# K through a bf16 staging tile, and W2 loaded behind the transposes of chunk 1, in a two-layer attention and MLP kernel

## The chip, the cores and the metric

The kernel runs on one core of a Trainium2 chip. The metric is the device time of one execution in microseconds (us). Five engines work beside each other, each on its own queue in order: PE (TensorE, matmuls; its weight loads are shown apart as PEld), DVE (VectorE), ACT (ScalarE), POOL (GpSimd) and SP (SyncE, which here only issues DMAs). DVE and ACT read PSUM, where matmuls leave their results; POOL works on SBUF alone. A measurement of this kernel can tell about 0.3% from no change.

## The reference

Two blocks, A (attention in a sliding window) and B (an MLP), each on a layer norm of x and added to x, applied as A, B, A, B. x is 2048 rows by 512, in bf16. Cut to what matters:

```python
def _A_ref(x, wqkv, wo):           # H = 32 heads, Dh = 16, window W = 256
    q, k, v = split(x @ wqkv)      # (heads, 2048, 16) each
    scores = einsum("bhqd,bhkd->bhqk", q, k) * Dh ** -0.5
    mask = (i - j >= 0) & (i - j < W)
    p = softmax(where(mask, scores, -1e9))
    return einsum("bhqk,bhkd->bhqd", p, v) @ wo
def _B_ref(x, w1, w2):             # 512 -> 1792 -> 512
    return relu(x @ w1) @ w2
x = x + _A_ref(_layernorm(x), A_wqkv, A_wo)
x = x + _B_ref(_layernorm(x), B_w1, B_w2)
x = x + _A_ref(_layernorm(x), A_wqkv, A_wo)
x = x + _B_ref(_layernorm(x), B_w1, B_w2)
```

## The kernel before

**Chunks and steps.** The 2048 rows are four chunks of 512. With two layers that makes eight steps, k = 0 to 7; step k is chunk k % 4 of layer k // 4. In each step the rows are normed, transposed, multiplied into Q, K and V, attended to, multiplied by wo, added to x, normed again, transposed, and sent through w1, relu and w2.

**K and its spread.** K of a step is made transposed, as four tiles t of 128 channels (8 heads of 16) by 512 keys. A score matmul contracts 32 channels, that is two heads, and must keep their scores apart. So K is stored twice in the tile `KBD`: once with the odd heads' channels set to zero, once with the even ones'. `spread_k` (L324) does this with a per-partition factor `par` of 0 or 1: two instructions for a tile of 512 keys, that read the matmul's PSUM result in fp32 and write bf16 into slots of 64 keys. There are 20 slots, used in a ring; where a tile goes over the ring's end, each of the two instructions becomes two of 256 keys. In step 0 the rows come in two halves, and its K instructions cover 256 keys.

**V.** V is copied from PSUM into a bf16 staging tile `Vst` on DVE or ACT, and from there `spread_v` (L336) lays it out by parity into `V2f` on POOL or DVE. The staging tiles come from the pool `stg`, which has three buffers; the output rows `ob` of layer 1 use the same pool.

**Attention.** Scores of a group go to PSUM (`Sps`), ACT takes their exponential into `Pb`, masks are set to zero in `Pb` on POOL (`affine_select`, two instructions per block) or DVE (`min` with `tri`), and PE multiplies the result by V (`acc`). DVE divides (`chk`, `O`). The four DMA transposes `OT<-O` then bring O back to the layout for wo. The normed rows `xn` (three buffers, on DVE or POOL) are turned by DMA transposes, too: `xnT<-xn` for Q, K, V and `xn2T<-xn` for w1. In step 0, and in the last step behind O and its norm, PE does the transposes.

**Who orders the work.** Nothing is issued in the order of the source. Every piece of work is an `op` with a key (its urgency), the engines that may do it with a cost for each, and the ops it waits for. A small event loop in the kernel's Python (`choose`, `begin`, L718 to L757) gives each free engine the best op that it may start, and so writes the program: one fixed queue per engine, and the engine for each op. On the chip the queues then run in this order, and an engine that waits holds everything behind it. Where the loop sees PE idle it puts in a `warm` matmul with no use for its result. PE's results pass through four PSUM buffers (the pool `psum`); a buffer comes free when its last reader is done. K, Q and V of step k + 1 are due 16 score groups ahead of that step's first scores.

**Loads.** All loads are issued by SP at the start, in this order: x of chunk 0 in two parts, wqkv in three, x of chunks 1 to 3, wo, w1, w2. The two weights of the MLP, 1792 KB each, are both called `w` in the profile. Behind the loads stand SP's transposes, chunk 1's four `xnT<-xn` first. All of them use one DMA queue, spread over 16 DMA engines.

All instructions that the loop places are recorded by one helper and so carry its line, L106; they are told apart by their tiles.

Of the kernel before, what the change touches and what calls it, by code (L numbers as in the profile page):

```python
# [10 lines left out]
BF16 = mybir.dt.bfloat16  # L11
I32 = mybir.dt.int32
AX = mybir.AxisListType
ACT = mybir.ActivationFunctionType
ALU = mybir.AluOpType
P = 128
# [46 lines left out]
def kernel(  # L63
# [51 lines left out]
    pe, dve, act, pool, sp = (InOrder(x) for x in (nc.tensor, nc.vector, nc.scalar, nc.gpsimd, nc.sync))  # L115
# [23 lines left out]
    w1 = const.tile([P, KC, DFF], BF16, name="w1")  # L139
    sp.dma_start(w1[:], B_w1.rearrange("(kc p) n -> p kc n", p=P))  # L140
    w2 = const.tile([P, NF, D], BF16, name="w2")
    sp.dma_start(w2[:], B_w2.rearrange("(f p) n -> p f n", p=P))


    ident = const.tile([P, P], BF16, name="ident")
# [9 lines left out]
    par = const.tile([P, 2], FP32, name="par")  # L155
# [31 lines left out]
    SOON = {"qkv": 0, "v": 0, "h": 0, "mask": 0, "div": -1, "add": -1}  # L187
# [34 lines left out]
    def op(key, opts, deps=(), take=None, uses=(), keep=0):  # L222
        uses = list(uses) + ([take] if take is not None and take not in uses else [])
        return Op(key, opts, deps, take, uses, keep)
# [3 lines left out]
    stg = Pool("stg", 3, work)  # L228
    ots = Pool("OT", 3, work)

    def landed(t):
        o = Op(0, {}, [], None, [], 0)
        fixed.append((o, t))
        return o
# [2 lines left out]
    d_x = [landed(3.95), landed(4.5)]  # L237
    d_w = {1: landed(7.4), 0: landed(9.0), 2: landed(10.6)}
    d_xc = {c: landed(11.4 + 1.7 * c) for c in range(1, NCH)}
    d_wo, d_w1, d_w2 = landed(18.0), landed(24.0), landed(30.0)  # L240


    def copy(e, o, i, relu=False):
        if e == "ACT":
            act.activation(o, i, ACT.Relu if relu else ACT.Copy)
        elif e == "POOL":
            pool.tensor_copy(o, i)
        elif relu:
            dve.tensor_relu(o, i)
        else:  # L250
            dve.tensor_copy(o, i)
# [3 lines left out]
    def options(times, fn):  # L255
        return {e: (t, lambda e=e: fn(e)) for e, t in times.items()}
# [67 lines left out]
    def spread_k(e, layer, c, t, h0, h1, ps):  # L324
        s0 = slot(layer, 8 * c)
        for a, b in ([(h0, h1)] if s0 + h1 <= NSLOT or s0 + h0 >= NSLOT else [(h0, NSLOT - s0), (NSLOT - s0, h1)]):
            sa = (s0 + a) % NSLOT
            for p in range(2):
                o = KBD[:, t, sa:sa + b - a, p, :]
                i = ps[:, 64 * a:64 * b].rearrange("p (s k) -> p s k", k=64)  # L330
                if e == "ACT":
                    act.activation(o, i, ACT.Copy, scale=par[:, p:p + 1])
                else:
                    dve.tensor_scalar(out=o, in0=i, scalar1=par[:, p:p + 1], scalar2=None, op0=ALU.mult)

    def spread_v(e, layer, c, j, src):  # L336
        v4 = src.rearrange("p (a e d) -> p e a d", e=2, d=16)
# [124 lines left out]
    def plan_qkv(k):  # L462
        layer, c = divmod(k, NCH)
        xnTs[k] = xnT = [None]
        src = [x_raw(4 * c + j, 4 * c + j + 1)[:, 0, :] if layer == 0 else x_sb[:, 4 * c + j, :] for j in range(4)]
        lid = 2 * k
        st, dst = [], []
        calm = (-10, 1, 40, 60)[k] if k < 4 else 0
        for j in range(4):
            came = [d_x[j // 2] if c == 0 else d_xc[c]] if layer == 0 else [x_done[k - 4, j]]  # L470
            st.append(norm_stats(lid, j, src[j], came + applied.get(lid - 8, []), j - 1 if j % 2 else None, calm))
        pw = [norm_pow(lid, j, j + 2, [st[j], st[j + 1]], calm - 5) for j in (0, 2)]
        free = [] if k == 1 else qkv_mm.get(k - 1, []) + (qkv_mm[0] if k == 2 else [])

        class Late:
            def __getitem__(self, i):
                if xnT[0] is None:
                    xnT[0] = work.tile([P, KC, 512], BF16, name="xnT", tag="hT" if k == 1 else "xnT", bufs=1)
                return xnT[0]
        for j in range(4):  # L480
            dst.append(norm_apply(lid, j, src[j], [pw[j // 2]], k == 0, Late(), -5000, free))
        applied[lid] = list(dst)
        mine = qkv_mm[k] = []
        old = [scores[s] for n in units_of.get(k - 2, []) for s in range(first_slot[n], first_slot[n] + len(units[n].groups))]
        old_pv = [pvs[n, j] for n in units_of.get(k - 2, []) for j in range(units[n].nq // 2)]
        wait = 0 if k == 0 else 16
        for h in range(2) if k == 0 else (None,):
            cols = slice(0, 512) if h is None else slice(256 * h, 256 * h + 256)
            h0, h1 = (0, 8) if h is None else (4 * h, 4 * h + 4)
            us = 0.216 if h is None else 0.115  # L490
            need_x = dst if h is None else dst[2 * h:2 * h + 2]
            w = 512 if h is None else 256
            for t in range(4):
                at = first_slot[units_of[k][t + 4 * (h or 0)]] - wait
                idx = 4 * k + t

                def kmm(kc, ps, t=t, cols=cols):
                    mm(ps[:, cols], wqkv[:, kc, D + t * P:D + (t + 1) * P], xnT[0][:, kc, cols], kc == 0, kc == KC - 1)
                box, m = group(at, KC, us, kmm, need_x + [d_w[1]] + old[len(old) * t // 4:len(old) * (t + 1) // 4], lead=1000)
                times = {"DVE": 1.46, "ACT": 1.42} if h is None else {"DVE": 0.87, "ACT": 0.83}  # L500
                k_done[k, t, h or 0] = op(SOON["qkv"], options(times, lambda e, t=t, h0=h0, h1=h1, box=box:
                                                      spread_k(e, layer, c, t, h0, h1, box.ps)),
                                          [m, c_par], None, [box])

                def qmm(kc, ps, t=t, cols=cols):
                    mm(ps[:, cols], wqkv[:, kc, t * P:(t + 1) * P], xnT[0][:, kc, cols], kc == 0, kc == KC - 1)
                last_use = [scores[s] for n, u in enumerate(units) if 4 * u.k + u.t == idx - 7
                            for s in range(first_slot[n], first_slot[n] + len(u.groups))]
                box, m2 = group(at + 0.1, KC, us, qmm, need_x + [d_w[0]] + last_use, lead=1000)

                def qev(e, t=t, cols=cols, box=box, idx=idx):
                    q = first(Q, (k, t), lambda: work.tile([P, 512], BF16, name="Qt", tag=f"Q{idx % 7}", bufs=1))
                    copy(e, q[:, cols], box.ps[:, cols])
                q_done[k, t, h or 0] = op(SOON["qkv"], options(EVAC[w], qev), [m2], None, [box])
                mine += [m, m2]
        for j in range(4):
            at = first_slot[units_of[k][0]] + (1 + (8 if j > 1 else 0) if k == 0 else 1.6 * j - wait)

            def vmm(kc, ps, j=j):
                mm(ps[:], xnT[0][:, kc, j * P:(j + 1) * P], wqkv[:, kc, 2 * D:3 * D], kc == 0, kc == KC - 1)  # L520
            box, m = group(at + 0.2, KC, 0.216, vmm, ([dst[j]] if k == 0 else dst) + [d_w[2]] + old_pv, lead=1000)
            vs = Box(stg)

            def vev(e, box=box, vs=vs):
                vs.t = vs.tile([P, 512], BF16, "Vst")
                copy(e, vs.t[:], box.ps[:])
            ev = op(SOON["qkv"], options(EVAC[512], vev), [m], vs, [box, vs])
            v_done[k, j] = op(SOON["v"], options({"POOL": 1.72, "DVE": 1.42} if k else {"POOL": 1.72, "DVE": 1.42, "ACT": 1.48}, lambda e, j=j, vs=vs: spread_v(e, layer, c, j, vs.t[:])),
                              [ev] + c_v, None, [vs])
            mine.append(m)  # L530
# [142 lines left out]
    for k in range(NSTEP):  # L673
        plan_attention(k)
        if k == 0:
            plan_qkv(1)
        plan_rest(k)
        if 0 < k < NSTEP - 1:
            plan_qkv(k + 1)
# [32 lines left out]
        push(t, None, None)  # L712
    started, score_end, idle_since, log = set(), [0.0], [1.9], []
    score_next = [0]

    by_name = {"PE": pe, "ACT": act, "DVE": dve, "POOL": pool, "SP": sp}

    def choose(e, t):  # L718
        best = None
# [153 lines left out]
    with tc.If(flag > 0):  # L873
# [13 lines left out]
        for layer in range(2):  # L887
            for c in range(NCH):
# [3 lines left out]
                for t in range(4):  # L892
                    q = work.tile([P, 512], BF16, name="Qt", tag=f"Q{t}", bufs=1)
                    Qts.append(q)
                    whole(KC, lambda kc, ps: mm(ps[:], wqkv[:, kc, t * P:(t + 1) * P], xnT[:, kc, :], kc == 0, kc == KC - 1),
                          lambda ps: nc.vector.tensor_copy(q[:], ps[:]))
                    whole(KC, lambda kc, ps: mm(ps[:], wqkv[:, kc, D + t * P:D + (t + 1) * P], xnT[:, kc, :], kc == 0, kc == KC - 1),
                          lambda ps: spread_k("DVE", layer, c, t, 0, 8, ps))
                for j in range(4):
                    whole(KC, lambda kc, ps: mm(ps[:], xnT[:, kc, j * P:(j + 1) * P], wqkv[:, kc, 2 * D:3 * D], kc == 0, kc == KC - 1),  # L900
                          lambda ps: spread_v("DVE", layer, c, j, ps[:]))
# [52 lines left out]
```

## Time and profile before

| | |
|---|---|
| median of 9 runs | 488.7 us (486.64 to 489.61) |
| profiled execution, its own time | 488.88 us |
| span of the profiled execution | 487.2 us |
| busy: PE, DVE, ACT, POOL | 463.8, 368.7, 337.7, 317.6 us |
| granted TensorE clock, mean over the span | 0.995 |
| K from PSUM into KBD on DVE, 512 keys, 256 keys | 40 of 741 ns, 42 of 476 ns |
| K from PSUM into KBD on ACT, 256 keys | 6 of 474 ns |
| V from staging on POOL, on DVE | 64 of 418 ns, 64 of 376 ns |
| masks on POOL | 526 of 433 ns |

The profiled execution takes 1.7 us more than its span, for what lies before the first and behind the last instruction; it is 0.2 us above the median. Busy time is the share of the span in which an engine had an instruction of the kernel under way. In a timeline a row is a run of equal instructions with its start, its length and, in brackets, the idle time of the engine just ahead of it and what ended it; a releaser is inferred, and where a wait has several conditions the one named is the last that the profile shows.

### The profile page before, as it was taken

The numbers are of one execution on the slowest core, as the hardware profiler recorded it, in microseconds if no ns is written. First come the engines' busy times: TensorE is split into PE (matmuls) and PEld (weight loads), VectorE is DVE, ScalarE is ACT, GpSimd is POOL, SyncE is SP. The second block draws the span as 40 slices with busy tenths as digits, with TensorE's granted clock in tenths as the row PEclk, the third lists the DMA queues.
The fourth block names the chain that finished last, engine by engine and source line by source line (L and its number), as shares of the span: only waits on it lengthen the run. The fifth ranks groups of instructions, "written<-read, shape, count | busy, mean of one in ns | idle before, by whom it ended". The sixth has DMA issues, their size and how long they took to land.

```text
span 487.2 us, 14677 instructions
## 1 busy us (share of the span) xinstructions
PE 463.8 (95%) x6055; PEld 249.5 (51%) x6055; DVE 368.7 (76%) x965; ACT 337.7 (69%) x281; POOL 317.6 (65%) x716
## 2 busy tenths in 40 slices
PE   7879899998999999999999999999999999999995
PEld 3544555654445545554544554555555455554662
DVE  6979989858898789877989977898668878463111
ACT  3858877878777868876778887777875676655340
POOL 7768878768886778866878767577656557631000
PEclk9989999999999999999999999999999999999999
DMA  8951141003300143002221114020153002100100
GB/s 258 370 65 23 27 64 24 3 1 57 67 12 3 21 69 45 3 1 44 56 36 23 23 28 52 12 44 3 24 88 56 13 1 46 34 12 13 34 23 28
DMA packets 54651, 22.00 MB, mean 45 GB/s; under 512 B 46128, under 2 KB 54064, under 8 KB 54576
## 3 DMA queue, kind: packets, MB, share of 16 engines
q1 hardware_dynamic: 54576, 20.98, 20.5%
q8 instruction: 49, 0.80, 0.7%
q14 instruction: 26, 0.21, 0.2%
HBM read 7.86 MB, written 2.10 MB: 20 GB/s over the span
## 4 chain that ended last, share of the span: by engine, by line
PE 73%; DVE 13%; DMA 8%; POOL 2%; ACT 2%; issue 1%; DVEq 0%; ACTq 0%; POOLq 0%
PE ps_d L106 52%; PE acc L106 12%; PE Sps L106 8%; DMA OT<-O 5%; DVE st L106 2%; DMA xnT<-xn 2%; DVE KBD L106 2%; ACT Pb L106 2%; DVE x_sb L106 1%; DVE xn L106 1%; DVE Pb L106 1%; DVE V2f L106 1%; DMA xn2T<-xn 1%; POOL Pb L106 1%; DVE O L106 1%
## 5 line engine op out<-in xcount | busy, mean ns | idle before, releaser
L106 ACT ACTIVATE Pb<-Sps 128x2048 bf16<-128x2048 f32 (+4 forms) x164 | 284.0, 1732 | 97.3 <-PE Sps L106 74.1
L106 POOL TENSOR_SCALAR_AFFINE_SELECT Pb<-Pb 64x256 bf16<-64x256 bf16 x526 | 227.8, 433 | 96.8 <-ACT Pb L106 74.2
L106 PE MATMUL ps_d<-xn2T,w 128*128 128x512 bf16 (+1 forms) x560 | 110.5, 337 | 1.3 <-DVE hT L106 1.0
L106 PE MATMUL ps_d<-w,hT 128*128 128x512 bf16 x448 | 110.0, 380 | 0.0
L106 PEld LDWEIGHTS <-Pb 128*128 128x128 bf16 x2880 | 83.3, 96 | 24.7 <-issue 7.3
L106 PE MATMUL acc<-V2f,Pb 128*128 128x34 bf16 x2880 | 89.9, 178 | 2.3 <-DVE Pb L106 1.1
L106 PE MATMUL ps_d<-xnT,wqkv 128*128 128x512 bf16 (+1 forms) x288 | 67.9, 362 | 3.9 <-DVE O L106 2.1
L106 PEld LDWEIGHTS <-w 128*128 128x128 bf16 x560 | 50.8, 97 | 39.7 <-issue 4.4
L106 PE MATMUL Sps<-Qt,KBD 32*128 32x192 bf16 (+4 forms) x1536 | 62.4, 249 | 2.6 <-ACT Pb L106 2.4
L106 DVE TENSOR_TENSOR Pb<-Pb,tri 128x512 bf16<-128x512 bf16 (+1 forms) x136 | 58.7, 436 | 6.7 <-ACT Pb L106 6.5
L106 PEld LDWEIGHTS <-hT 128*128 128x128 bf16 x448 | 40.0, 97 | 44.2 <-issue 2.8
L106 DVE TENSOR_SCALAR hT<-ps_d 128x512 bf16<-128x512 f32 (+1 forms) x76 | 47.0, 626 | 11.1 <-PE ps_d L106 10.5
L106 PEld LDWEIGHTS <-KBD 32*128 32x128 bf16 x1536 | 25.6, 92 | 53.5 <-issue 50.4
L106 DVE TENSOR_SCALAR KBD<-ps_d,par 128x256 bf16<-128x256 f32 (+1 forms) x82 | 45.5, 605 | 1.1 <-PE ps_d L106 0.9
L106 ACT ACTIVATE hT<-ps_d 128x256 bf16<-128x256 f32 (+1 forms) x64 | 29.6, 466 | 22.7 <-PE ps_d L106 21.1
L106 DVE BATCH_NORM_STATS2 st<-x_sb 128x6 f32<-128x512 f32 (+1 forms) x64 | 43.7, 683 | 1.5 <-DMA x_sb<-in_A_x_dram 1.1
L106 DVE TENSOR_TENSOR x_sb<-ps_d,x_sb 128x512 f32<-128x512 f32 x48 | 32.8, 685 | 14.5 <-PE ps_d L106 14.1
L106 PEld LDWEIGHTS <-wqkv 128*128 128x128 bf16 x288 | 26.4, 99 | 28.6 <-issue 5.9
L106 DVE TENSOR_TENSOR O<-acc,chk 128x128 bf16<-128x128 f32 x128 | 37.3, 292 | 4.4
L106 DVE RECIPROCAL chk<-acc 128x8 f32<-128x8 f32 x128 | 25.7, 201 | 18.4 <-PE acc L106 16.0
L106 PE MATMUL ps_d<-wo,OT 128*128 128x512 bf16 x128 | 32.7, 380 | 4.4 <-DMA OT<-O 4.2
L106 DVE TENSOR_TENSOR ob<-ps_d,x_sb 128x512 bf16<-128x512 f32 x16 | 11.0, 689 | 31.5 <-PE ps_d L106 31.5
(55 smaller groups left out, 299.9 us busy)
## 6 DMA issues: line engine op xcount, KB each, us to landing
w<-in_B_w_dram SPq DMA_DIRECT2D x2, 1792.0 KB, 13.6
out_dram<-ob SPq DMA_DIRECT2D x16, 128.0 KB, 1.7
wqkv<-in_A_wqkv_dram SPq DMA_DIRECT2D x3, 512.0 KB, 7.5
x_sb<-in_A_x_dram SPq DMA_DIRECT2D x3, 512.0 KB, 9.4
x_sb<-in_A_x_dram SPq DMA_DIRECT2D x2, 256.0 KB, 3.3
wo<-in_A_wo_dram SPq DMA_DIRECT2D x1, 512.0 KB, 8.8
xnT<-xn SPq DMA_TRANSPOSE x28, 2.5
OT<-O SPq DMA_TRANSPOSE x28, 2.5
```

The source lines that it names most:

```text
L106: inst = fn(*a, **k)
```

## The change

Two things are changed, and the event loop then writes a new order for all engines.

K of steps 1 to 7 is first copied from PSUM by one instruction on DVE or ACT into a bf16 staging tile `Kst`, from the same three `stg` buffers that V uses. `spread_k` then reads `Kst` instead of PSUM, and may run on DVE or POOL. In step 0 the spread from PSUM stays, on DVE or ACT.

The load of w2 leaves its place at the start. It becomes an `op` on SP that waits for the four transposes `xnT<-xn` of chunk 1 (`applied[2]`), and w2's first matmuls wait for it in the loop's planning, where they had a fixed time before.

```diff
     w2 = const.tile([P, NF, D], BF16, name="w2")
-    sp.dma_start(w2[:], B_w2.rearrange("(f p) n -> p f n", p=P))
...
-    d_wo, d_w1, d_w2 = landed(18.0), landed(24.0), landed(30.0)
+    d_wo, d_w1 = landed(18.0), landed(24.0)
+    by_name = {"PE": pe, "ACT": act, "DVE": dve, "POOL": pool, "SP": sp}
...
                 if e == "ACT":
                     act.activation(o, i, ACT.Copy, scale=par[:, p:p + 1])
                 else:
-                    dve.tensor_scalar(out=o, in0=i, scalar1=par[:, p:p + 1], scalar2=None, op0=ALU.mult)
+                    by_name[e].tensor_scalar(out=o, in0=i, scalar1=par[:, p:p + 1], scalar2=None, op0=ALU.mult)
...
                 times = {"DVE": 1.46, "ACT": 1.42} if h is None else {"DVE": 0.87, "ACT": 0.83}
-                k_done[k, t, h or 0] = op(SOON["qkv"], options(times, lambda e, t=t, h0=h0, h1=h1, box=box:
-                                                      spread_k(e, layer, c, t, h0, h1, box.ps)),
-                                          [m, c_par], None, [box])
+                if k == 0:
+                    k_done[k, t, h or 0] = op(SOON["qkv"], options(times, lambda e, t=t, h0=h0, h1=h1, box=box:
+                                                                   spread_k(e, layer, c, t, h0, h1, box.ps[:])),
+                                              [m, c_par], None, [box])
+                else:
+                    ks = Box(stg)
+
+                    def kev(e, box=box, ks=ks):
+                        ks.t = ks.tile([P, 512], BF16, "Kst")
+                        copy(e, ks.t[:], box.ps[:])
+                    ev = op(SOON["qkv"], options(EVAC[512], kev), [m], ks, [box, ks])
+                    k_done[k, t, 0] = op(SOON["qkv"], options({"DVE": 0.8, "POOL": 1.3}, lambda e, t=t, ks=ks:
+                                                              spread_k(e, layer, c, t, 0, 8, ks.t[:])),
+                                         [ev, c_par], None, [ks])
...
         if k == 0:
             plan_qkv(1)
+            d_w2 = op(0, {"SP": (1.4, lambda: sp.dma_start(w2[:], B_w2.rearrange("(f p) n -> p f n", p=P)), 9.0)}, applied[2])
         plan_rest(k)
```

## The prediction

> **What bounds the kernel now.** I read the page first, for the busy shares and the chain that ended last.
>
> ```profile
> PE 463.8 (95%) x6055; PEld 249.5 (51%) x6055; DVE 368.7 (76%) x965; ACT 337.7 (69%) x281; POOL 317.6 (65%) x716
> PE 73%; DVE 13%; DMA 8%; POOL 2%; ACT 2%; issue 1%; DVEq 0%; ACTq 0%; POOLq 0%
> ```
>
> PE is the bound. Its work is the same after the change (the same matmuls, bar the `warm` fillers), so the change is worth what it takes from PE's idle time, 487.2 - 463.8 = 23.4 us, from fillers, and from slowed matmuls. Idle time saved early reaches the end: the last stage is a solid row of PE matmuls, and no load is late by then.
>
> Next I looked at PE's waits, and at the timelines of PE and DVE around the longest of them.
>
> ```profile
> PE ps_d L106 <- DMA OT<-O: 4.2, 6, 1.1
> PE ps_d L106 <- DVE O L106: 2.1, 1, 2.1
> PE acc L106 <- DVE Pb L106: 1.1, 1, 1.1
> PE acc L106 <- POOL Pb L106: 1.0, 2, 0.7
> PE ps_d L106 <- DVE hT L106: 1.0, 2, 0.8
> PE ps_d L106 <- DVE KBD L106: 0.4, 1, 0.4
> ```
>
> ```profile
> 26.46 0.38 PE L106 MATMUL Sps<-Qt,KBD 32*128 32x64 bf16 x12 [0.45 <-ACT Pb L106]
> 28.97 2.72 PE L106 MATMUL ps_d<-xnT,wqkv 128*128 128x256 bf16 x12 [2.13 <-DVE O L106]
> ```
>
> ```profile
> 28.06 0.41 DVE L106 TENSOR_SCALAR xn<-x_sb,mvs,rstds 128x512 bf16<-128x512 bf16 x1 [2.59 <-DMA xnT<-xn]
> ```
>
> PE's longest single wait in mid-run is 2.13 us at 26.8 us: it wants a PSUM buffer that DVE's divide has yet to release. DVE is late because just before it sat 2.59 us, waiting to write the fourth `xn` of chunk 1 into a staging buffer that the first transpose `xnT<-xn` had not finished reading. That transpose was issued at 21.79 and landed at 28.03 (21.79 plus 6.24 in the chain); the median of all 28 is 2.5 (the page's DMA issues, below, with the two weight loads and the windows of 28 to 32 us).
>
> ```profile
> 21.79 6.24 DMA xnT<-xn
> ```
>
> ```profile
> w<-in_B_w_dram SPq DMA_DIRECT2D x2, 1792.0 KB, 13.6
> ...
> xnT<-xn SPq DMA_TRANSPOSE x28, 2.5
> ```
>
> ```profile
> 28.00:30.00 2.00, 1.03 (x6) 0.72 (x6) 1.87 (x7) 0.60 (x1) 1.76 (x5) 0.62 0.30 57
> 30.00:32.00 2.00, 2.00 (x20) 1.19 (x18) 1.91 (x6) 0.38 (x1) 1.74 (x5) 0.52 0.19 36
> ```
>
> What stood ahead of it is w2. The two weight loads were issued at 9.80 and 11.71 and took 12.1 and 15.1 us (the ends of the `w` tile's answer, of median 13.6), so w1 landed at 21.9 and w2 at 26.8: 1792 KB in 4.9 us. After the wait PE's clock was granted at 0.62 and 0.52 for four microseconds (the column before the last two of the last two lines), a second cost of the same stall.
>
> **Part 1: w2 behind the transposes.** In the changed program every engine's order up to some 33 us is the old one, except that SP issues w2 after the fourth `xnT<-xn`. So this stretch can be costed row by row. The first transpose is then behind w1 alone (landed 21.9, when it was issued) and lands near 21.8 + 2.5 = 24.3; DVE reaches the fourth `xn` at 25.5 and does not wait. DVE gains 2.59, and PE's 2.13 goes with it: the divide that PE needs ends at 28.91 - 2.59 = 26.3, before PE asks at 26.84. Without that gap I expect no slow clock. The row at 28.97 took 2.72 for 12 matmuls of 256 columns; 12 such elsewhere take 1.49 (at 58.02), so 1.23 is saved there and 0.12 on the scores behind (0.52 against 0.40 for 12). PE could gain 2.13 + 1.35 = 3.5. But DVE is nearly full here (3.78 of the 4 us from 28 to 32), so the gain cannot much exceed DVE's own: 2.59 plus its next wait for PE, 0.57, is 3.16. I take -3.2; the ends are -2.6 (DVE's wait alone) and -3.8 (0.3 more on PE, if the gap at 34.6 closes too).
>
> What is late next: PE reaches chunk 1's K at about 28.9 (32.69 less 3.8), and its fourth transpose, issued near 25.9, lands near 28.4. That costs nothing, at most 0.5. w2 is issued near 27.1; SP takes 1.4 to 1.9 us for it, and 4.9 us of transfer behind a start-up of about 2 (a first load of 256 KB lands 3.3 us after its issue) put its landing near 34. Its first matmul ran at 66.26, so w2 itself is never waited for. But SP's next items are the two `OT<-O` of chunk 0, issued at 35.76 before and now 3 us earlier, so the first one may stand behind w2's tail, and DVE's `O` behind nothing new. The first wo then waits 0 to 1.5 us; in the old order its transpose had landed 1.3 before its use (38.17 against 39.45). I take +0.3.
>
> **Part 2: K by way of a staging tile.** Counts are from the two programs, durations from the rows of the trace.
>
> Removed, steps 1 to 7: on DVE 40 x 0.741 + 28 x 0.476 = 43.0 us; on ACT 4 x 0.474 = 1.9. Added: 13 copies on DVE x 0.684 (its cast of V) = 8.9; 15 on ACT x 0.595 = 8.9; spreads of 512 keys, 32 on DVE and 8 on POOL, and of 256 keys, 16 on each. A bf16 multiply from SBUF by a per-partition scalar is not in the trace. On DVE the nearest row is the bf16 `xn`, 0.383 to 0.58, mean 0.42; from below the fastest V copy of 256 elements, 0.215; from above K's own 0.741. I take 0.42, and 0.27 for 256 keys (the same ratio as 476 to 741). On POOL the nearest is the bf16 `xn`, 0.77 to 1.13, mean 0.84, and for 256 the V copy, 0.42. So DVE +13.4 +4.3 and POOL +6.7 +6.7.
>
> The reordering moves more: 24 V copies go from POOL to DVE (+9.0, -10.0), 8 Q copies from ACT to DVE (+5.4, -4.8), 7 V casts the other way (-4.8, +4.2), 14 mask instructions leave POOL (-6.1) and 7 mask instructions come to DVE (+2.4). With small items DVE ends at -4, ACT +7, POOL -4 us. None of them bounds: the largest is DVE with 369 of 487. All this is covered by PE's matmuls; the cover is gone where a score waits for `KBD`. PE's wait for K is 0.4 on `ps_d` in this trace, and K is due 16 score groups early, each with an exponential of some 1.9 us, so two instructions in place of one have about 30 us of slack. Added waits: an ACT or DVE copy now waits for one of three `stg` buffers shared with V, and on ACT the next exponential stands behind it, on DVE the next mask; a late POOL spread holds both. Bounds: from below, all small PE waits for masks, hT and K vanish (1.1 + 1.0 + 1.0 + 0.4 = 3.5 less); from above, each of the 8 POOL spreads once delays PE by the longest POOL wait seen (8 x 0.7 = 5.6 more). Engines that were not the bound change by under 2%, so I take 0.
>
> The Trainium skill speaks against this part. "SBUF — State Buffer", section "Who interferes with whom", says that a VectorE scalar multiply in a two-port mode and a GpSimd instruction cannot share their SBUF port pair: whichever comes second stands until the first ends. The trace agrees that something like it happens: DVE's V copies take 215 to 472 ns, and POOL's masks 408 to 715. By that rule, as an estimate, each of the 48 new DVE multiplies meets a running POOL instruction in 65% of cases and waits half of its 0.43 us, 6.8 us in all, and POOL waits as much; by the rows, DVE's waiting is in the 0.42 already. If a tenth of POOL's share reached PE, the sum would be 0.7 us worse by the rule; if all of it did, 6.8.
>
> **Planned holes.** The changed program holds 35 fillers against 38: 2 in place of 8 while chunk 1's first scores run, 11 in place of 8 near 105 to 125 us. The eight took 1.90 us at 53.19, 0.24 each, so 3 fewer are -0.7; bounds -1.6 (with the 0.89 gap beside them) and +0.7, if the new holes are longer than planned.
>
> **Sum.** -3.2 + 0.3 + 0 - 0.7 = -3.6 us. The profiled execution took 488.88 (span 487.2 and 1.7 around it), so 485.3; it is 0.2 above the median of 488.7, so the median becomes 485.1.
>
> **Rivals.**
>
> - Slower: POOL's spreads come late. Place: the PV matmuls, which wait for masks queued on POOL behind a K spread of two to four instructions (1.7 us). For it: POOL is busy 86% of 36 to 60 us (20.66 of 24). Against: PE waits only 1.0 us for POOL in the whole run, and POOL's own total falls. At the bound of +5.6 the time is 485.1 + 5.6 = 490.7; it decides above +5.1, where 490.2, 0.3% over 488.7, is passed.
> - No difference: the early gain is taken back by chunk 1's exponentials and the chain behind wo. For it: from 51 to 57 us PE waited for ACT (0.89, 0.19) and ran fillers, a stage in which being earlier means only waiting longer. Against: what comes before ACT there moves up too. With only the 0.7 of fewer fillers left, 488.0.
> - More: copies free PSUM buffers in 0.6 to 0.7 us where a spread held them 1.5, and the small waits go as well: 485.1 - 3.5 = 481.6.
>
> **Chances.** Forecast (483.0 to 487.2) 0.56; more gained 0.16; no difference 0.15; slower 0.13. Within 0.3% of 488.7, that is 487.2 to 490.2, a measurement can't tell from no change. Faster is then 0.72, same 0.15, slower 0.13. The range 481.5 to 489.5 leaves out about 0.15 of the slower case and a little of the gain beyond all small waits.
>
> **What would show it.** Right: the first `xnT<-xn` lands within 3 us of its issue, DVE's 2.59 and PE's 2.13 are gone, the clock stays at 1.00 from 28 to 32 us, everything at 36 us is some 3 us earlier, PE's total idle falls by about 2 to 3 us; K spreads on DVE take about 0.42 us. Wrong: a first wait for `OT<-O` over 1.5 us at 36 us; ACT waiting for a POOL `KBD`; PE waits for `Pb` from POOL well over 1.0 us; a second stretch of low clock near the fillers at 105 to 125 us.

## The result: 1.3% slower, and where the profile after shows it

The changed kernel takes 494.42 us (median of 10 runs, 492.56 to 496.75), the kernel before 487.94 (31 runs): a ratio of 1.0129, interval 1.0113 to 1.0145. The forecast was 485.1, faster. The profiled execution of the changed kernel took 492.36, just below the lowest of the others; its span is 490.2.

From the page after, the busy shares and the chain by engine:

```profile
PE 463.9 (95%) x6052; PEld 249.8 (51%) x6052; DVE 365.9 (75%) x992; ACT 343.9 (70%) x290; POOL 330.8 (67%) x699
PE 72%; POOL 15%; DMA 3%; DVE 3%; ACT 3%; issue 2%; POOLq 0%; ACTq 0%; DVEq 0%
```

PE's work is what it was. DVE, at 13% of the chain before, has 3%, and POOL has gone from 2% to 15%: POOL's busy time rose by 13 us (317.6 to 330.8), where the prediction had it fall by 4.

The first half of the change did its work. The timelines of SP and PE after, at the place where PE waited 2.13 us before:

```profile
21.42 5.40 SPq L106 DMA_TRANSPOSE xnT<-xn  x4
26.87 0.58 SPq L106 DMA_DIRECT2D w<-in_B_w_dram  x1
32.59 2.50 SPq L106 DMA_TRANSPOSE OT<-O  x2
```

```profile
26.09 0.37 PE L106 MATMUL Sps<-Qt,KBD 32*128 32x64 bf16 x12 [0.45 <-ACT Pb L106]
26.39 1.52 PE L106 MATMUL ps_d<-xnT,wqkv 128*128 128x256 bf16 x12
```

The four transposes stand in a row, w2 behind them; the 12 matmuls that took 2.72 us after a wait of 2.13 take 1.52 with no wait, and the transposes of O start at 32.59 where they started at 35.76, 3.2 us earlier. All of that, and more, is lost in the next 30 us: the first matmul with w2 starts at 67.99, where it started at 66.26. PE's waits after:

```profile
PE ps_d L106 <- DMA OT<-O: 4.4, 3, 2.7
PE ps_d L106 <- DVE hT L106: 4.1, 1, 4.1
PE acc L106 <- POOL Pb L106: 3.6, 7, 0.9
PE acc L106 <- POOL V2f L106: 1.5, 2, 0.8
```

One new wait of 4.1 us, the waits for POOL's masks up from 1.0 to 3.6, a new one for POOL's V copies, and a 2.7 in place of a 1.1 for a transpose of O. The long one is read from the timelines of PE, DVE and POOL, in the order in which they wait for each other:

```profile
63.59 1.01 PE L106 MATMUL ps_d<-xn2T,w 128*128 128x256 bf16 x4 [4.08 <-DVE hT L106]
```

```profile
62.25 0.96 DVE L106 TENSOR_SCALAR xn<-x_sb,mvs,rstds 128x512 bf16<-128x512 bf16 x2 [4.47 <-POOL rstds L106]
63.14 1.93 DVE L106 TENSOR_SCALAR hT<-ps_d 128x256 bf16<-128x256 f32 x5
```

```profile
51.85 6.20 POOL L106 TENSOR_SCALAR KBD<-Kst,par 128x512 bf16<-128x512 bf16 x4
58.01 0.73 POOL L106 TENSOR_TENSOR rstds<-rstds,mhalf 128x2 f32<-128x2 f32 x1
...
59.44 0.77 POOL L106 TENSOR_SCALAR xn<-x_sb,rstds,nbs 128x512 bf16<-128x512 bf16 x1
...
61.50 0.72 POOL L106 TENSOR_TENSOR rstds<-rstds,mhalf 128x2 f32<-128x2 f32 x1
```

PE wants a PSUM buffer that DVE's `hT` has yet to empty; DVE stands before it, waiting 4.47 us to apply a norm (`xn`, of chunk 2) whose scale `rstds` comes from POOL; and POOL is late because the spreads of two K tiles ahead of it, four instructions, took 6.20 us. Behind the wait PE's clock is low, as the windows after show (the column ahead of the last two is the granted clock):

```profile
60.00:63.00 3.00, 0.00 (x0) 0.00 (x0) 0.75 (x2) 0.51 (x1) 2.75 (x7) 1.00 0.30 59
63.00:67.00 4.00, 3.41 (x63) 2.56 (x63) 3.52 (x12) 0.88 (x1) 3.38 (x9) 0.57 0.45 87
```

0.57 over 4 us is 1.7 us of PE's time gone ((1 - 0.57) x 4), on top of the wait. The rows of the spread itself, among the groups by shape after:

```profile
L106 POOL TENSOR_SCALAR KBD<-Kst,par 128x256 bf16<-128x256 bf16 x16 | 15.1, 956 | 0.1
L106 DVE TENSOR_SCALAR KBD<-Kst,par 128x512 bf16<-128x512 bf16 x32 | 13.7, 468 | 0.1
L106 POOL TENSOR_SCALAR KBD<-Kst,par 128x512 bf16<-128x512 bf16 x8 | 13.0, 1640 | 0.3
```

On POOL the multiply takes 1640 ns for 512 keys and 956 for 256, twice what I took from the nearest rows (840 and 420). A tile takes 3.3 us and more, where the event loop was told 1.3.

**The theory** from this: P, the POOL spread costs twice what was thought, so the written order has POOL too early in it, and what stands behind the spreads is late; w2's move is good. The rivals: W, the move of w2 is what hurts; L, the new spreads on DVE and POOL's instructions obstruct each other.

### The profile page after: what moved, and what is told of

The parts are those of the page before. It is cut to its first block, busy times and chain, and to the rows that moved or that the text cites. A ratio compares the mean times of both kernels' runs of the same rounds, so it can differ in the third digit from the quotient of the medians.

```text
span 490.2 us, 14698 instructions
## 1 busy us (share of the span) xinstructions
PE 463.9 (95%) x6052; PEld 249.8 (51%) x6052; DVE 365.9 (75%) x992; ACT 343.9 (70%) x290; POOL 330.8 (67%) x699
## 4 chain that ended last, share of the span: by engine, by line
PE 72%; POOL 15%; DMA 3%; DVE 3%; ACT 3%; issue 2%; POOLq 0%; ACTq 0%; DVEq 0%
PE ps_d L106 52%; PE acc L106 12%; PE Sps L106 8%; POOL Pb L106 7%; POOL KBD L106 3%; ACT Pb L106 2%; DMA OT<-O 2%; POOL V2f L106 2%; POOL xn L106 1%; POOL rstds L106 1%; DVE st L106 1%; POOL nbs L106 1%; DMA x_sb<-in_A_x_dram 1%; DMA xnT<-xn 1%; DVE xn L106 1%
## 5 line engine op out<-in xcount | busy, mean ns | idle before, releaser
L106 POOL TENSOR_SCALAR_AFFINE_SELECT Pb<-Pb 64x256 bf16<-64x256 bf16 x512 | 223.3, 436 | 89.8 <-ACT Pb L106 68.1
L106 PE MATMUL acc<-V2f,Pb 128*128 128x34 bf16 x2880 | 91.1, 178 | 5.2 <-POOL Pb L106 3.6
L106 PE MATMUL ps_d<-xnT,wqkv 128*128 128x512 bf16 (+1 forms) x288 | 66.4, 356 | 1.1 <-ACT KBD L106 0.9
L106 DVE TENSOR_SCALAR hT<-ps_d 128x512 bf16<-128x512 f32 (+1 forms) x77 | 47.1, 615 | 10.9 <-PE ps_d L106 9.8
L106 DVE RECIPROCAL chk<-acc 128x8 f32<-128x8 f32 x128 | 25.9, 203 | 21.7 <-PE acc L106 19.3
L106 PEld LDWEIGHTS <-wqkv 128*128 128x128 bf16 x288 | 25.9, 97 | 25.7 <-issue 3.3
L106 PE MATMUL ps_d<-wqkv,xnT 128*128 128x512 bf16 x128 | 34.1, 379 | 0.1
```

Of the source, the lines that this page charges most:

```text
L106: inst = fn(*a, **k)
```

## The experiments

All ratios are to the kernel before on the same chip in the same call, with their 95% intervals. The event loop wrote the same order for all engines but SP with and without w2's move (in the traces the rows of DVE, ACT, POOL and the weight loads stand in the same order), so the two halves can be had apart without any other difference.

| run | median us | ratio to before |
|---|---|---|
| changed kernel | 494.42 | 1.0129 (1.0113 to 1.0145) |
| w2_alone | 484.51 | 0.9949 (0.9932 to 0.9965) |
| k_alone | 497.96 | 1.0208 (1.0169 to 1.0247) |
| pool_two_op | 484.90 | 0.9952 (0.9936 to 0.9969) |
| two_op_step1 | 488.83 | 1.0029 (1.0012 to 1.0047) |
| two_op_later | 490.22 | 1.0063 (1.0046 to 1.0080) |
| pool_const | 492.11 | one run |
| true_costs | 485.02 | 0.9965 (0.9946 to 0.9984) |
| dve_only | 482.53 | 0.9913 (0.9888 to 0.9938) |
| two_op_replanned | 489.10 | 1.0035 (1.0020 to 1.0049) |
| dve_only_095 | 486.93 | 0.9990 (0.9973 to 1.0008) |
| dve_only_ot36 | 482.86 | 0.9927 (0.9901 to 0.9954) |

**The two halves.** The kernel before with w2's load moved, and the changed kernel with it put back:

```diff
 # w2_alone, on the kernel before
-    sp.dma_start(w2[:], ...)
+            d_w2 = op(0, {"SP": (1.4, lambda: sp.dma_start(w2[:], ...), 9.0)}, applied[2])
 # k_alone, on the changed kernel
+    sp.dma_start(w2[:], ...)
-            d_w2 = op(0, {"SP": (1.4, lambda: sp.dma_start(w2[:], ...), 9.0)}, applied[2])
```

> The kernel before with only the load of w2 moved behind the four transposes of chunk 1; every other queue keeps its order. Theory P (the POOL spreads cost twice what was planned and estimated; w2's move does what the prediction said): 2.6 to 3.8 us faster than before, about 484.7, with DVE's 2.59 us and PE's 2.13 us gone. Rival W (w2's move is what hurts): at or above 490.

> The changed kernel with w2 loaded at the start as before; all other queues are those of the changed kernel. Theory P: slower than the changed kernel by about w2's 3 us, some 497, with the POOL spread at 1.6 us for 512 keys and the 4 us wait of PE still there. Rival W: back near 488.

w2 alone is 0.51% faster, 2.6 us in its call; K alone is 2.1% slower, 10.9 us. Rival W is out. The product of the two ratios, 1.0156, and the whole change at 1.0129 agree within the intervals. In k_alone the spread on POOL takes 1609 ns for 512 keys and PE's wait for `hT` is 4.4 us, as in the changed kernel. The old wait is back too, longer than before, and the clock is low in three places (timeline of PE, then windows):

```profile
29.79 1.44 PE L106 MATMUL ps_d<-xnT,wqkv 128*128 128x256 bf16 x6 [3.28 <-DVE O L106]
```

```profile
29.00:33.00 4.00, 3.21 (x25) 1.89 (x25) 3.68 (x12) 0.38 (x1) 2.21 (x6) 0.59 0.19 37
...
67.00:71.00 4.00, 3.37 (x64) 2.58 (x64) 3.52 (x12) 0.84 (x1) 3.41 (x9) 0.57 0.46 89
132.00:136.00 4.00, 4.00 (x23) 1.28 (x22) 2.92 (x7) 1.88 (x1) 0.82 (x2) 0.57 0.17 33
```

**The price of the POOL spread, with the order kept.** POOL's norm applies two operations in one instruction and takes 0.77 us for 512 elements at best (59.44 in POOL's timeline above); the spread has one operation. So the spread was given a second, adding zero. No queue's order changes.

```diff
-                    by_name[e].tensor_scalar(out=o, in0=i, scalar1=par[:, p:p + 1], scalar2=None, op0=ALU.mult)
+                    pool.tensor_scalar(out=o, in0=i, scalar1=par[:, p:p + 1], scalar2=0.0, op0=ALU.mult, op1=ALU.add)
```

> The changed kernel with all queues as they are; POOL's spread multiplies by the same 0 or 1 and then adds 0.0 in the same instruction, as the POOL norm with its two operations takes 0.77 us for 512 elements where the spread with one takes 1.57. If the one-operation form is what is slow, the 512-key spread falls to some 0.8 us, and by theory P the time falls to 485 to 488 with the order of work unchanged. If it stays at 1.6 us, the time stays at 494 and the cause of the price is elsewhere (the pattern of the destination, say).

Its groups by shape, and PE at the place of the 4 us wait:

```profile
L106 POOL TENSOR_SCALAR KBD<-Kst,par 128x256 bf16<-128x256 bf16 x16 | 8.4, 537 | 0.1
L106 POOL TENSOR_SCALAR KBD<-Kst,par 128x512 bf16<-128x512 bf16 x8 | 5.4, 693 | 0.3
```

```profile
58.82 0.60 PE L106 MATMUL ps_d<-xn2T,w 128*128 128x256 bf16 x4 [1.02 <-DVE hT L106]
```

More arithmetic takes less than half the time: 693 ns in place of 1640. With nothing else changed the kernel goes from 1.0129 to 0.9952, 1.8% or 8.6 us, to just below the 485 to 488 that was expected. That shows P: the length of 24 POOL instructions is the whole loss. With it gone the change stands where w2_alone stands (484.90 and 484.51 in the same call), so K by way of staging is worth nothing either way in this order. A part of the 8.6 us is the clock: its mean over the executions is 0.989 in the changed kernel and 0.996 here, which over 490 us is some 3.6 us (an estimate from these two means).

**Where the loss sits.** The fast form for the three tiles of step 1 alone, or for the five later tiles alone:

```diff
 # two_op_step1; two_op_later has (layer, c) != (0, 1)
-                elif e == "POOL":
+                elif e == "POOL" and layer == 0 and c == 1:
```

> The changed kernel with all queues as they are; the two-operation form of POOL's spread is used for the three tiles of step 1 alone (9.7 us of POOL's time before, some 4.1 with it), the five later tiles keep the slow form. Theory P, with the loss in one place (POOL late by some 4 us at 58 us, the norm behind it late, DVE and PE waiting 4 us, a slow clock after it): the wait of 4.1 us and the slow clock behind it go, 494.4 becomes 487 to 489. Rival: the loss is spread over all eight tiles, then three eighths of 9.5 us come back, 491.

> The counterpart of the run with the fast form in step 1 alone: all queues of the changed kernel, POOL's spread in the fast form in steps 2 to 7 (five tiles) and in the slow form in step 1 (three tiles). If the losses of the two places add up, this stands at about 0.8% below the changed kernel (the fast form everywhere won 1.8%, step 1 alone 1.0%), 490 to 491, with the 4 us wait at 59 us still there. If the later tiles cost nothing by themselves, it stays at 494.

Step 1 alone brings 1.00% (4.9 us), the later tiles 0.66% (3.2 us); together 1.66 of the 1.77. Both times lie in the ranges that were expected, but neither "in one place" nor "evenly over the tiles" is right: step 1 holds more than half of the loss, and its three tiles are three eighths of all. By POOL's time it is plainer still: the fast form takes 5.6 us off POOL's work in step 1 and 8.7 off the later tiles. In two_op_step1 the wait at 58 us is 0.91; 4.08 - 0.91 of wait and the 1.7 of slow clock add up to the 4.9. Other waits moved as well (for POOL's masks from 3.6 to 1.4, for ACT's exponentials from 1.3 to 2.7), so that sum explains the size and doesn't prove it.

In two_op_later the wait of step 1 is shorter than in the changed kernel, though nothing ahead of it differs. It ends at the same time, 63.6 us; PE only came to it 1.5 us later, since the clock was granted at 0.50 from 55 to 58 us. The 17 matmuls that take 2.03 us in the changed kernel take 3.69:

```profile
54.45 3.69 PE L106 MATMUL ps_d<-xn2T,w 128*128 128x256 bf16 x17
...
63.64 0.60 PE L106 MATMUL ps_d<-xn2T,w 128*128 128x256 bf16 x4 [2.56 <-DVE hT L106]
```

**What the slow form is.** One operation by a constant in place of the scalar per partition (this leaves the parity out of the tiles that POOL spreads):

```diff
-                    by_name[e].tensor_scalar(out=o, in0=i, scalar1=par[:, p:p + 1], scalar2=None, op0=ALU.mult)
+                    pool.tensor_scalar(out=o, in0=i, scalar1=0.5, scalar2=None, op0=ALU.mult)
```

> The changed kernel with all queues as they are; POOL's spread is one multiply by a constant 0.5 in place of the per-partition scalar, so the parity is left out and the scores of those tiles mix two heads. It asks only what the slow form is: if the one operation is slow, the 512-key instruction stays at 1.6 us; if it is the per-partition scalar in a one-operation instruction, it falls to 0.7 to 0.8.

Its groups by shape:

```profile
L106 POOL TENSOR_SCALAR KBD<-Kst 128x256 bf16<-128x256 bf16 x16 | 13.6, 872 | 0.1
L106 POOL TENSOR_SCALAR KBD<-Kst 128x512 bf16<-128x512 bf16 x8 | 11.9, 1508 | 0.3
```

1508 ns: the scalar per partition is not what is slow, the one-operation multiply is. Why a single operation takes twice as long there is not shown by any run.

**Telling the loop the true price.** The slow form stays, but is planned as what it is:

```diff
-options({"DVE": 0.8, "POOL": 1.3}, ...
+options({"DVE": 0.95, "POOL": 3.3}, ...
```

> The changed kernel with the slow one-operation form on POOL, but the event loop is told 3.3 for it in place of 1.3 (and 0.95 in place of 0.8 for DVE); it still gives 7 of the 28 tiles to POOL, in other places. If what hurts is that the order was written for a POOL that is 2 us per tile faster, the time is 482 to 486, as with DVE alone. If POOL's extra work itself hurts, wherever it stands, it stays above 490.

0.9965, 485.02: POOL still spends 25.9 us on spreads (6 of 1775 ns and 16 of 971; 28.1 in the changed kernel), but where the loop placed them they cost little. So POOL's extra work by itself is not what hurts; it hurts in an order written for a faster POOL. This order is a new one for all engines, though, and as the last three runs show, that alone can move the time by some 4 us; the gain of 8 us is twice that.

**DVE alone.** No spread on POOL, 72 instructions on DVE:

```diff
-options({"DVE": 0.8, "POOL": 1.3}, ...
+options({"DVE": 0.8}, ...
```

> The changed kernel, but the spread from staging runs on DVE alone (28 tiles in 72 instructions, against 48 on DVE and 24 on POOL); the queues are written anew. Theory P: no POOL spread, no 4 us wait, so the gain of w2 shows: 483 to 487. Rival L (the DVE spreads from SBUF and POOL's masks stand in each other's way, and that is what makes masks late): no better than the changed kernel, 494 or more, since there are half as many again of them on DVE.

482.53, 0.9913: the fastest of all, half a microsecond below the range that was expected, and faster than both kernels. Rival L falls at the size that it would need: half as many again of the DVE spreads, and masks on POOL take 436 ns as in the changed kernel (433 before). Something of it is there in the small. Of the 40 DVE spreads of 512 keys in this run, the 31 that start while POOL has an instruction under way take 503 ns in the median, the other 9 take 351. That the two engines hold each other up is a likely reading, but no run shows it.

**How much an order is worth by itself.** Three runs in which only what the loop is told differs, and with it the order and which engine does what:

```diff
 # two_op_replanned, on pool_two_op
-{"DVE": 0.8, "POOL": 1.3}
+{"DVE": 0.95, "POOL": 1.5}
 # dve_only_095, on dve_only
-{"DVE": 0.8}
+{"DVE": 0.95}
 # dve_only_ot36, on dve_only: the transposes OT<-O
-..., 2.6)}
+..., 3.6)}
```

> The two-operation form on POOL, and the event loop told 1.5 for it and 0.95 for DVE. If a fast spread on two engines is worth more than on DVE alone, below 482.5; theory P expects 481 to 485, since neither engine bounds.

> The spread on DVE alone, with 0.95 in place of 0.8 told to the event loop, nearer to what two instructions of 0.47 take. No instruction changes, only the order and which engine does what. Theory P says nothing of it beyond 481 to 485. If a newly written order moves the time by several us whatever the reason, as the replanned two-operation run hints (4 us slower than the same instructions in the other order), it may lie anywhere from 481 to 489.

> The spread on DVE alone, with 3.6 in place of 2.6 told to the event loop for the transposes of O (those issued closely behind others land 3 to 4.8 us after their issue). If the 2.6 us wait for O's transposes near 117 us, which all new orders show, comes from that too small figure, it shrinks, and the time falls below 482.5; otherwise 482 to 486.

The first missed: told costs nearer to the measured ones, it is 0.83% (4.0 us) slower than the same forms in the old order. The second is 0.77% (3.8 us) slower than dve_only, with no instruction's form changed. The third shrank the wait it was meant for, from 2.6 to 1.2 us, and won nothing, so it missed too. So a new order can move the time by some 4 us, whatever the reason for writing it, and the 2.0 us between dve_only and w2_alone are not shown to be the merit of the staging.

A part of this is the clock. dve_only and two_op_replanned both have a wait of 2.6 us for a transpose of O that begins between 117 and 119 us; the windows behind it, of dve_only and then of two_op_replanned:

```profile
120.00:124.00 4.00, 3.95 (x28) 1.51 (x29) 2.88 (x7) 1.72 (x1) 1.78 (x4) 1.00 0.34 66
```

```profile
120.00:124.00 4.00, 3.09 (x18) 0.91 (x19) 1.21 (x4) 0.12 (x1) 3.22 (x9) 0.50 0.47 79
124.00:128.00 4.00, 3.95 (x40) 1.92 (x40) 2.66 (x8) 2.56 (x2) 0.97 (x2) 0.65 0.48 94
```

No slow clock in one, 3.4 us lost in the other ((1 - 0.50) x 4 + (1 - 0.65) x 4), after a wait of the same length. The Trainium skill, "TensorE: Matmul & The Clock Gate", Part 1, says that the clock is set by PE's activity in free-running windows of 3413 ns: half speed after an idle window, full speed after a busy one. The lengths here agree: 0.57 over 4 us, as in the windows further up, is 3.4 us at half clock, and the 3.4 us lost here are 6.8 us at half clock, two windows. The condition does not: these low clocks follow waits of 2.1 to 4.4 us, most of them shorter than a window, and in two_op_later the 0.50 from 55 to 58 us follows no single PE wait above 0.9 us. What sets the low clock off is therefore not shown by these runs, only that it can come after a wait and need not.

## Why the prediction was wrong, by its own steps

- **Part 1, w2 behind the transposes: right in the mechanism, somewhat high in the sum.** DVE's 2.59 us and PE's 2.13 went, the clock held 1.00 from 28 to 32 us, O's first transposes came 3.2 us earlier (2.8 in w2_alone). I took -3.2 and +0.3, so -2.9; w2 alone measured -2.6 (0.51%, at most 0.7%). The two small terms were the wrong way round. The +0.3 for the transposes of O behind w2 was not there: in w2_alone w2 landed at 34.9, O's two transposes took the usual 2.5 us and the first wo did not wait (in the changed kernel the first of the two took 3.1, and the first wo did not wait either). What I had put at nothing, the fourth `xnT<-xn`, landed at 29.9 and not at 28.4, and PE's first row that reads all four starts at 30.0 after a wait of 0.47 us (the profile names a mask on DVE as its end, so the transpose's share is not shown).
- **Part 2, the price of the spread on POOL: the step that failed.** Part 2 entered the sum as 0; it was +8.6 us, all of it by the length of POOL's spreads (pool_two_op). I wrote that on POOL "the nearest is the bf16 `xn`, 0.77 to 1.13, mean 0.84", and the V copy for 256 keys. That row has two operations in one instruction, and the copy has none; the spread has one, and took 1.64 and 0.96. POOL +13.4 us became +28.1, and POOL's total rose by 13 where I had -4. My price for POOL came from rows of other forms, and had no upper end. The norm's bf16 rows, 0.835 on POOL and 0.440 on DVE, would have given a factor of 1.9, and with K's own 0.741 on DVE an end of 1.4 us, as an estimate.
- **"Engines that were not the bound change by under 2%, so I take 0": the second half of the step, and wrong as a rule.** POOL is at 67% of the span and yet delays PE by 4 us in one place, because each queue is fixed and one that is late holds what stands behind. I had looked at the slack of `KBD`, due 16 groups early; the work that waited was not K but the norm behind it on POOL's queue.
- **The upper bound, 8 x 0.7 = 5.6, was too small.** It measured a delay of PE by the longest wait for POOL in the trace of before, 0.7 us; one place alone brought a wait of 4.08. The length of POOL's spreads costs 8.6 us, and K alone 10.9 in its call.
- **The slower rival had the mechanism and not the place.** It said that POOL's spreads come late, and looked for it at the masks. The masks did cost more (1.0 to 3.6 us), but the largest piece went by way of `rstds`, DVE's `xn` and `hT`. It was given 0.13 and a price of +5.6 at most; the time of 494.4 lay beyond it. The working named this sign in advance (waits for POOL, and a second stretch of low clock), and both are there, the low clock at 63 us and not near the fillers.
- **DVE's spread** took 0.468 and 0.332 against 0.42 and 0.27, 11% and 23% more; too little to matter. The row that I took it from has a mean of 0.440, not 0.42.
- **The shared port rule** was weighed at 0.7 to 6.8 us. DVE's spreads are longer beside a busy POOL (503 ns against 351, above), but no run shows a loss of that size; dve_only, with the most DVE spreads, is the fastest.
- **Planned holes, -0.7:** not measured by itself, and smaller than what any new order moves.

## What to carry to other kernels

Price an instruction on the engine where it will run, in its own form: two forms of the same arithmetic differed by more than two here, and the one with more operations was the faster. Where queues are fixed by a planner, a wrong cost on an engine with a third of its time to spare still stalls the bounding engine, since its lateness falls on whatever stands behind it; ask not whether the engine bounds but what is next in its queue. And measure the parts of a change apart before judging either: here one half won 0.5% and the other lost 2%, and a zero added to the second would have kept the gain.

## What the runs showed of the hardware that I had not expected

- A multiply of bf16 in SBUF on POOL takes 1640 ns for 512 elements with one operation (1508 by a constant), and 693 ns with a second operation that adds zero; for 256 elements 956, 872 and 537.
- A PE wait of 2.6 us is followed by a granted clock of 0.50 and 0.65 over 8 us in one run, and of 1.00 in another.
- The same queues with the same waits up to 0.9 us ran at a clock of 1.00 from 55 to 58 us in the changed kernel and at 0.50 in two_op_later.
